# New durations in the planner of a fused linear-attention and two-MLP kernel

## The chip, the cores and the metric

The kernel runs on one core of a Trainium2 chip. Its time is the device time of one execution in microseconds (us). Before the change three runs took 1206.03, 1209.85 and 1210.98 us; the median is 1209.85 us. The profile is of one more execution, which took 1209.43 us.

## The reference

A recurrent attention over 4 x 8 heads, 768 steps, head size 40, feeds an MLP, and that feeds a second MLP. All is float32.

```python
for t in range(S):                      # state: B x H x D x D
    y[:, :, t] = einsum('bhd,bhde->bhe', r_t, state)
    Sa = einsum('bhde,bhe->bhd', state, a_t)
    state = state * w_t - outer(Sa, b_t) + outer(v_t, k_t)
x = y as 3072 tokens x 320
x = square(relu(x @ w_in))  @ w_out     # 320 -> 2048 -> 320
x = square(relu(x @ w_in2)) @ w_out2
```

## The kernel before

**The work.** The attention is computed in chunks of 32 steps. A slot n holds two such chunks (64 steps) of half of the batch; there are 24 slots. For each pair of slots the vector engine makes decay products with scans (`keys`, written into `w`, `sp`, `mm` or `kt`), multiplies them into `x` and `kb`, inverts small triangular matrices (`invert`: a block transpose into `p`, a first product from `lq` and `p`, fifteen steps on `mm`, a block transpose into `tt`), and transposes `kb` into `kt` (`values`). `chain` is the recurrence: for each of the two chunks of a slot TensorE runs small matmuls in the order `q,x` (result read out to `ss`), `ss,tt`, `q,lk`, `cs,q`, `r,ss`, each waiting for a copy or product of the one before on ScalarE or VectorE.

MLP 1 works on blocks of 256 tokens, one block for each pair of slots, 12 in all; MLP 2 has 12 blocks of the same size. A block has 16 steps. In MLP 1 a step is eight matmuls on `m_xh`, `m_xl` (in-step), a gate on ScalarE (relu, square, a rounding cast into `m_h`; the remainder `m_l` is made on VectorE or GpSimd), and eight matmuls on `m_h`, `m_l` (out-step). So each number is carried as two rounded parts. In MLP 2 the out-step has six matmuls of 320 columns. The weights come as raw 64-bit words and are decoded on the chip: `decode_w1` at the start, beside the first attention slots, and `decode_w2` after the last attention instruction, because the second weights lie where the attention's tiles lay. A decoded chunk takes two ScalarE multiplies and a rounding copy, three bit operations on VectorE, and two or three sums and products on VectorE or GpSimd.

**What sets the order.** All calls go through a recorder, `_Plan`. It keeps for each engine the time at which it would be free, by a table of costs, and gives the engine that is free first its ready task of the lowest priority number. Attention has the slot's number, the decode of the weights 2.7, gates -200, MLP matmuls 1000 and more: MLP matmuls fill the time in which no attention matmul is ready. The costs thus decide how many MLP matmuls stand between two attention groups in TensorE's queue, which the chip then runs strictly in that order. `cost` gives the time of a call on VectorE, ScalarE or GpSimd, `array` the cycles of a group of matmuls, `pe_time` turns these into time with a model of the clock, `taken` models the port that VectorE and GpSimd share. `either` records a call that two engines could do; `run` gives it to one of them by the same times. `plan.run("att")` plans until the last attention task; only then are the tasks of `decode_w2` and MLP 2 added.

Of the kernel before, what the change touches and what calls it, by code (L numbers as in the profile page):

```python
# [12 lines left out]
U32 = mybir.dt.uint32  # L13
# [59 lines left out]
class _Plan:  # L73
# [65 lines left out]
    def cost(self, eng, op, outs, ins):  # L139
        o = outs[0]  # L140
        n = 1
        for _, c in o.ap[1:]:
            n *= c
        if eng == "SP":
            return 690.0 if o.ap[0][1] in (32, 64) else 480.0
        psum = any(str(z.space).endswith("PSUM") for z in ins)
        if eng == "ACT":
            return (55 if psum else 93) + (90 if len(ins) > 1 else 0) + n / 1.2
        if eng == "POOL":
            return 149 + 2.1 * n if ins else 35 + 0.83 * n  # L150
        if op == "reciprocal":
            return 70 + n * 6.25
        if op == "tensor_reduce":
            n = 1
            for _, c in ins[0].ap[1:]:
                n *= c
        if op in ("tensor_copy", "tensor_scalar") and not psum:
            n /= 2
        return (64 + n) / 0.96

# [12 lines left out]
    def op(self, eng, name, fn, outs, ins, kw):  # L173
        cost = (2.0 if "is_transpose" in kw else 4.0) if eng.name == "PE" else self.cost(eng.name, name, outs, ins)
        rec = (eng.name, fn, cost, outs, ins, self.ports(eng.name, name, outs, ins))
        if self.open is not None:
            self.open.append(rec)
        else:
            self.add([rec])
# [12 lines left out]
    def add(self, ops, alts=None):  # L192
# [26 lines left out]
        if eng == "SP":  # L219
# [5 lines left out]
            nbytes *= max(1.0, 512 / run)  # L225
        k = self.array(ops) if eng == "PE" else None
        alts = alts or {eng: ([o[1] for o in ops], cost, max(o[5] for o in ops))}
        self.tasks.append((alts, self.prio, nbytes, self.tag, k))
        self.left[self.tag] = self.left.get(self.tag, 0) + 1
# [18 lines left out]
    def array(self, ops):  # L248

        cycles, columns, tiles, mode = 0, 0.0, [], None  # L250
        for _, _, passes, outs, ins, _ in ops:
            k, m = ins[0].ap[0][1], ins[0].ap[1][1]
            n = 1
            for _, c in outs[0].ap[1:]:
                n *= c
            r0, c0 = ins[0].offset // ins[0].ap[0][0], outs[0].offset // outs[0].ap[0][0]
            rows = 32 if k <= 32 else 64 if k <= 64 else 128
            cols = 32 if m <= 32 else 64 if m <= 64 else 128
            if rows == 128:
                r0 = 0  # L260
            mode = (rows, cols)
            if ins[0].dtype == F32R:
                cycles += max(n, 2 * m) + 6
                columns += n * m / 128
                tiles = []
                continue
            tile_ = (r0, c0)
            clash = [z for z in tiles if not (z[0] != r0 or z[1] != c0)] or (
                rows == 128 and any(z[1] == c0 for z in tiles)
            )  # L270
            if tiles and not clash:
                cycles += passes / 2 * m
                columns += passes * n * m / 128
                tiles.append(tile_)
            else:
                cycles += passes * max(n, m)
                columns += passes * n * m / 128
                tiles = [tile_]
        return mode, cycles, columns
# [29 lines left out]
    def taken(self, e, port, t, cost):  # L309

        if not port or e not in ("DVE", "POOL"):
            return t
        other = "POOL" if e == "DVE" else "DVE"
        until, what = self.held.get(other, (0.0, 0))
        if e == "DVE" and (port == 2 or what == 1) or e == "POOL" and (what == 2 or port == 1):
            t = max(t, until)
        self.held[e] = (t + cost, port)
        return t
# [963 lines left out]
```

## Time and profile before

| | |
|---|---|
| profiled execution | 1209.43 us |
| span of its instructions | 1207.6 us |
| TensorE busy | 1104.0 us (91%) |
| VectorE busy | 805.9 us (67%) |
| ScalarE busy | 747.5 us (62%) |
| GpSimd busy | 388.2 us (32%) |

In the table of stretches further down, the time from 0 to 140 us holds the start and the decode of the first weights, 140 to 716 us attention with MLP 1 in its gaps, 716 to 870 us the rest of MLP 1 beside the decode of the second weights, and the rest MLP 2 alone. A busy TensorE is not TensorE at its peak: matmuls overlap, and so the mean time of one is longer than the time between two.

### The profile page before, as it was taken

To read this page: it belongs to the slowest core of one execution; us is meant where nothing else is said; L and a number is where in the kernel's file an instruction comes from. 1 tells how busy PE (TensorE), PEld (TensorE's weight loads), DVE (VectorE), ACT (ScalarE), POOL (GpSimd) and SP (SyncE) were. 2 spreads that over 40 slices of the span, in tenths; PEclk is the share of its full clock that TensorE was granted. 3 is DMA by queue.
4 is the path that set the end of the run, shared out by engine and by line. 5 is a ranking of instruction groups with operands and counts; after the bars stand their busy time and mean duration, and the time that the engine had idled before them with its cause. 6 is when DMAs were issued, how large, how long until landed. Compare 5 with 4: busy or idle time off the path is not lost.

```text
span 1207.6 us, 43193 instructions
## 1 busy us (share of the span) xinstructions
PE 1104.0 (91%) x18096; PEld 1032.2 (85%) x18096; DVE 805.9 (67%) x1786; ACT 747.5 (62%) x2077; POOL 388.2 (32%) x443
## 2 busy tenths in 40 slices
PE   3888898998989998899899999999899999999996
PEld 2656787887878887798789899999899999999996
DVE  6887888789888978999798746666773232222221
ACT  4496554555565565556446468888666666666664
POOL 7544334223323332343224117776820000000000
PEclk9986789999998999999899999999899999999999
DMA  8555343155325515533451322332241010101000
GB/s 244 143 154 146 85 104 103 57 127 146 79 70 138 136 49 127 143 90 78 123 121 36 60 74 84 93 93 82 79 140 36 25 29 24 33 24 27 13 12 14
DMA packets 142239, 103.86 MB, mean 86 GB/s; under 512 B 98001, under 2 KB 110162, under 8 KB 142034
## 3 DMA queue, kind: packets, MB, share of 16 engines
q1 hardware_dynamic: 142034, 101.00, 31.5%
q8 instruction: 144, 2.36, 0.8%
q14 instruction: 61, 0.50, 0.1%
HBM read 82.88 MB, written 11.80 MB: 78 GB/s over the span
## 4 chain that ended last, share of the span: by engine, by line
PE 50%; DVE 7%; ACT 3%; issue 2%; DMA 1%; POOL 1%; SPq 1%; DVEq 0%; ACTq 0%; POOLq 0%
PE bank L69 50%; DVE mm L69 3%; DVE q L69 2%; ACT mm L69 1%; ACT q L69 1%; SPq L69 1%; DVE x L69 0%; DVE y L69 0%; DVE kt L69 0%; ACT m_h L69 0%; DMA v<-in_el_dram 0%; POOL kb L69 0%; DMA lk<-kt 0%; DVE p L69 0%; DMA mm<-in_win_dram 0%
## 5 line engine op out<-in xcount | busy, mean ns | idle before, releaser
L69 PE MATMUL bank<-m_xh,wi 128*128 128x256 f32 x1920 | 387.0, 286 | 9.7 <-ACT mm L69 5.4
L69 POOL TENSOR_TENSOR m_l<-mm,m_h 128x256 fp32r<-128x256 f32 x200 | 162.8, 816 | 546.3 <-ACT m_h L69 293.7
L69 PEld LDWEIGHTS bank<-m_xh,wi 128*128 128x128 f32 x1920 | 315.3, 193 | 13.2 <-ACT mm L69 6.0
L69 PE MATMUL bank<-m_xl,wi 128*128 128x256 f32 x1152 | 324.2, 285 | 1.8 <-POOL m_xl L69 1.8
L69 ACT ACTIVATE mm<-bank 128x256 f32<-128x256 f32 x384 | 146.2, 382 | 233.1 <-PE bank L69 214.3
L69 DVE TENSOR_TENSOR m_l<-mm,m_h 128x256 fp32r<-128x256 f32 x184 | 85.0, 462 | 217.6 <-ACT m_h L69 209.7
L69 PEld LDWEIGHTS bank<-m_xl,wi 128*128 128x128 f32 x1152 | 222.3, 193 | 2.3 <-POOL m_xl L69 2.3
L69 ACT ACTIVATE mm<-mm 128x256 f32<-128x256 f32 (+3 forms) x500 | 205.0, 423 | 30.6 <-POOL m_xl L69 14.8
L69 PE MATMUL bank<-m_h,wo 128*128 128x256 f32 x960 | 206.7, 297 | 0.1
L69 PE MATMUL bank<-wo,m_h 128*128 128x320 f32 x768 | 172.5, 311 | 1.7 <-ACT m_h L69 1.2
L69 PEld LDWEIGHTS bank<-m_h,wo 128*128 128x128 f32 x960 | 156.6, 192 | 10.0 <-issue 1.4
L69 PE MATMUL bank<-m_l,wo 128*128 128x256 f32 x576 | 156.6, 284 | 0.1
L69 ACT CAST m_h<-mm 128x256 fp32r<-128x256 f32 x359 | 145.1, 405 | 10.2 <-PE bank L69 1.9
L69 PEld LDWEIGHTS bank<-wo,m_h 128*128 128x128 f32 x768 | 125.7, 190 | 2.2 <-ACT m_h L69 1.4
L69 PE MATMUL bank<-wo,m_l 128*128 128x320 f32 x384 | 119.2, 310 | 1.0 <-POOL m_l L69 1.0
L69 DVE TENSOR_TENSOR mm<-mm 128x30 f32<-128x30 f32 (+9 forms) x317 | 106.0, 334 | 8.4 <-ACT wi L69 0.7
L69 PEld LDWEIGHTS bank<-m_l,wo 128*128 128x128 f32 x576 | 110.7, 192 | 0.5 <-POOL m_l L69 0.3
L69 DVE TENSOR_TENSOR q<-bank,cs 32x128 f32<-32x128 f32 (+1 forms) x240 | 87.7, 366 | 30.6 <-ACT q L69 22.2
L69 PE MATMUL bank<-q,lk 128*40 128x72 f32 x1536 | 63.7, 233 | 23.7 <-DVE q L69 10.6
L69 PEld LDWEIGHTS bank<-q,lk 128*40 128x40 f32 x1536 | 53.7, 120 | 31.7 <-ACT mm L69 9.9
L69 ACT COPY q<-bank 40x256 f32<-40x256 f32 (+1 forms) x168 | 54.6, 325 | 37.3 <-PE bank L69 33.6
L69 ACT ACTIVATE q<-bank 32x160 f32<-32x160 f32 x192 | 56.6, 295 | 27.3 <-PE bank L69 24.8
(135 smaller groups left out, 1633.1 us busy)
## 6 DMA issues: line engine op xcount, KB each, us to landing
kb<-in_el_dram SPq DMA_DIRECT2D x24, 512.0 KB
mm<-in_win_dram SPq DMA_DIRECT2D x30, 256.0 KB
a<-in_el_dram SPq DMA_DIRECT2D x24, 256.0 KB
v<-in_el_dram SPq DMA_DIRECT2D x24, 256.0 KB
r<-in_er_dram SPq DMA_DIRECT2D x24, 256.0 KB
lk<-kt SPq DMA_DIRECT2D x96, 64.0 KB
mm<-in_wr_dram SPq DMA_DIRECT2D x20, 260.0 KB
mm<-in_wout_dram SPq DMA_DIRECT2D x20, 256.0 KB
```

The lines of the kernel that those rows point to most:

```text
L69: self.plan.op(self, op, lambda: getattr(self.real, op)(*args, **kw), outs, ins, kw)
```

## The change

A few numbers of the planner change. No instruction is added or taken away; their order on all five engines changes, and which engine does what `either` leaves open.

```diff
-        if op in ("tensor_copy", "tensor_scalar") and not psum:
+        if op == "tensor_tensor_scan":
+            n *= 2.15
+        elif op == "transpose":
+            n = max(1.09 * n, 1.85 * min(n, 512))
+        elif o.dtype == U32:
+            n *= 1.2
+        elif op in ("tensor_copy", "tensor_scalar") and not psum:
             n /= 2
         return (64 + n) / 0.96
...
             if ins[0].dtype == F32R:
-                cycles += max(n, 2 * m) + 6
+                cycles += max(n, 2 * m) + 30
```

By these lines an MLP matmul of 256 columns is planned with 286 cycles instead of 262, a scan of 520 elements with 1231 ns instead of 608, the transpose of 512 elements with 1053 ns instead of 600, and a bit operation on 256 elements with 387 ns instead of 200 (one input) or 333 (two inputs).

Three places of the new order follow. The first is VectorE at the fifth of the twelve inversions, from the block transpose into `p` on. Before:

```order
L69 STREAM_TRANSPOSE p_115<-l_113 128x1024
L69 TENSOR_TENSOR q0_111<-bank0_67,cs_66 32x4x32 x3
L69 TENSOR_TENSOR y1_122<-bank2_69,w0_102 104x4x32
L69 TENSOR_TENSOR mm_81<-lq_114,p_115 128x16x32
L69 TENSOR_TENSOR q0_111<-bank0_67,w2_104 40x4x40
L69 TENSOR_TENSOR x1_106<-bank3_70,cs_66 32x512
```

Now:

```order
L69 STREAM_TRANSPOSE p_115<-l_113 128x1024
L69 TENSOR_TENSOR q0_111<-bank0_67,w2_104 40x4x40
L69 TENSOR_TENSOR q0_111<-bank1_68,w2_104 40x4x40
L69 TENSOR_TENSOR y0_121<-bank0_67,w2_104 104x4x32
L69 TENSOR_TENSOR q0_111<-bank1_68,w2_104 40x4x40
L69 TENSOR_TENSOR y1_122<-bank2_69,w0_102 104x4x32
```

The product from `lq` and `p` has left VectorE. The second place is GpSimd at the same inversion. Before:

```order
L69 TENSOR_TENSOR m_xl0_85<-mm_81,m_xh0_83 128x768
L69 TENSOR_TENSOR m_l0_90<-mm_81,m_h0_87 128x256
L69 TENSOR_TENSOR p_115<-p_115,mm_81 128x16x32
L69 TENSOR_TENSOR m_l1_91<-mm_81,m_h1_88 128x256
L69 TENSOR_TENSOR x2_107<-a_96,w2_104 64x512
```

Now:

```order
L69 TENSOR_TENSOR m_xl0_85<-mm_81,m_xh0_83 128x768
L69 TENSOR_TENSOR m_l1_91<-mm_81,m_h1_88 128x256
L69 TENSOR_TENSOR mm_81<-lq_114,p_115 128x16x32
L69 TENSOR_TENSOR p_115<-p_115,mm_81 128x16x32
L69 TENSOR_TENSOR m_l2_92<-mm_81,m_h2_89 128x256
```

The product stands here now, ahead of the sum into `p` that needs it. The third place is TensorE in the middle of attention, at the group of transposing matmuls `cs,q` of an odd slot (`q1`). Before:

```order
L69 MATMUL bank5_72<-m_xh1_84,wi1_125 128x256
L69 MATMUL bank5_72<-m_xh1_84,wi3_1_126 128x256
L69 MATMUL bank5_72<-m_xl1_86,wi3_1_126 128x256
L69 MATMUL bank2_69<-cs_66,q1_112 40x40 x16
L69 MATMUL bank1_68<-q0_111,lk0_108 40x72 x8
L69 MATMUL bank3_70<-sp_116,kb0_98 32x32 x32
```

Now:

```order
L69 MATMUL bank1_68<-q1_112,lk1_109 40x72 x8
L69 MATMUL bank0_67<-q0_111,lk0_108 40x72 x8
L69 MATMUL bank6_73<-m_h2_89,wo1_127 128x256 x2
L69 MATMUL bank6_73<-m_l2_92,wo1_127 128x256
L69 MATMUL bank2_69<-cs_66,q1_112 40x40 x16
L69 MATMUL bank1_68<-q0_111,lk0_108 40x72 x8
```

Between the second half of `q1,lk1` and `cs,q1` there were sixteen MLP matmuls, of which the last three are shown; now there are three and a small group of the other slot. Counted over the whole order, 2064 MLP matmuls stood ahead of the last attention matmul, and now 2168 do. By the attention group that they stand directly ahead of, `x,kb` has 519 instead of 434, `q,lk` 638 instead of 566, `ss,tt` 446 instead of 416, `cs,q` 245 instead of 323. Up to the last attention instruction VectorE has 1393 calls instead of 1400: three products into `kb` fewer, two into `x`, four from `lq`, one into `p`, one `m_xl`, and casts (three `m_h`, one `m_xh`, one `wo`), but one product into `sp` more, one `m_l`, and seven read-outs (two and four into `q`, one into `ss`). GpSimd has 285 instead of 268, among them seven `m_l` more.

## Rows read from the trace of the kernel before

**Rows 1.** Windows: busy us of each engine, PE clock, DMA, five stretches.

```profile
core 0: us, PE busy (x) PEld busy (x) DVE busy (x) ACT busy (x) POOL busy (x), PEclk, DMA share, GB/s
0.00:140.00 140.00, 97.21 (x1638) 75.90 (x1638) 113.66 (x284) 85.11 (x242) 73.33 (x82) 0.86 0.60 165
140.00:677.00 537.00, 490.62 (x11900) 446.43 (x11900) 464.24 (x1052) 302.87 (x874) 176.17 (x200) 0.95 0.39 99
716.00:870.00 154.00, 149.28 (x1219) 147.38 (x1220) 96.44 (x174) 125.74 (x359) 109.41 (x128) 0.98 0.31 91
870.00:1199.00 329.00, 328.48 (x2483) 328.08 (x2482) 107.93 (x214) 213.44 (x544) 25.66 (x29) 0.99 0.13 35
```

**Rows 2.** Chain that ended last, 480 to 600 us, share by line.

```profile
by line: PE bank L69 37.7%; DVE mm L69 12.5%; DVE q L69 10.0%; issue 9.0%; ACT q L69 4.7%; SPq L69 4.4%; DVE x L69 3.5%; DMA v<-in_el_dram 3.4%; ACT mm L69 2.1%; DVE p L69 2.0%; DVE kt L69 1.9%; DMA mm<-ys 1.9%; DVE y L69 1.7%; POOL p L69 1
```

**Rows 3.** The same chain after 670 us: start, us, what.

```profile
677.62 69.34 PE bank L69 x1121
748.21 83.12 PE bank L69 x707
...
854.61 1.00 DVE wi L69
855.62 2.69 DMA mm<-in_win_dram
...
868.71 329.78 PE bank L69 x2487
```

**Rows 4.** Groups on PE, 140 to 716 us: count, busy, mean ns, idle before.

```profile
L69 PE MATMUL bank<-q,lk 128*40 128x72 f32 x1408 | 58.3, 232 | 21.8 <-DVE q L69 8.7 <-ACT m_h L69 4.4 <-ACT mm L69 3.2
...
L69 PE MATMUL bank<-cs,q 40*40 40x40 f32 x1344 | 33.8, 204 | 1.8 <-DVE y L69 1.6
L69 PE MATMUL bank<-ss,tt 32*32 32x72 f32 x1408 | 32.0, 235 | 5.0 <-issue 1.5 <-DVE ss L69 1.1 <-ACT ss L69 0.9
```

**Rows 5.** Tile `lk` on PE: duration min/median/max, first and last start.

```profile
L69 PE MATMUL bank<-q,lk x1536: 223/226/342, 76.2 to 715.7; 128*40 128x72 f32 x192
```

**Rows 6.** Windows of 20 us in and after the rest of MLP 1.

```profile
780.00:800.00 20.00, 20.00 (x173) 20.00 (x173) 13.65 (x26) 15.75 (x45) 13.53 (x17) 1.00 0.27 77
...
860.00:880.00 20.00, 16.07 (x84) 14.92 (x85) 15.71 (x24) 13.13 (x36) 14.63 (x16) 0.74 0.39 108
```

**Rows 7.** Groups on VectorE, whole span, by shape.

```profile
L69 DVE TENSOR_TENSOR x<-a,w 64x512 f32<-64x512 f32 x17 | 24.0, 1413 | 0.6
...
L69 DVE TENSOR_TENSOR kb<-kb,mm 128x512 f32<-128x512 f32 x18 | 20.2, 1122 | 0.2
...
L69 DVE CAST m_h<-mm 128x256 fp32r<-128x256 f32 x25 | 7.3, 292 | 9.7 <-ACT mm L69 9.3 <-issue 0.2
```

**Rows 8.** Tile `lq` by engine: duration min/median/max.

```profile
L69 POOL TENSOR_TENSOR mm<-lq,p x6: 1046/1049/1052, 171.6 to 646.4; 128x512 f32<-128x512 f32 x6
L69 DVE TENSOR_TENSOR mm<-lq,p x4: 681/924/1248, 279.7 to 492.8; 128x512 f32<-128x512 f32 x4
```

**Rows 9.** Groups on GpSimd, whole span, by shape.

```profile
L69 POOL TENSOR_TENSOR m_l<-mm,m_h 128x256 fp32r<-128x256 f32 x200 | 162.8, 816 | 546.3 <-ACT m_h L69 293.7 <-DVE m_h L69 139.4 <-issue 64.2
L69 POOL TENSOR_TENSOR kb<-kb,mm 128x512 f32<-128x512 f32 x22 | 31.2, 1421 | 0.1
L69 POOL TENSOR_TENSOR x<-a,w 64x512 f32<-64x512 f32 x21 | 26.0, 1239 | 54.4 <-DVE w L69 32.5 <-PE bank L69 20.5 <-DMA a<-in_el_dram 1.2
```

**Rows 10.** Groups on ScalarE, 716 to 870 us, by shape.

```profile
L69 ACT ACTIVATE mm<-mm 128x256 f32<-128x256 f32 x86 | 35.1, 418 | 1.7 <-DMA mm<-in_win_dram 0.8
L69 ACT CAST m_h<-mm 128x256 fp32r<-128x256 f32 x76 | 30.5, 403 | 1.1 <-PE bank L69 0.2
L69 ACT ACTIVATE mm<-bank 128x256 f32<-128x256 f32 x77 | 29.1, 380 | 21.7 <-PE bank L69 17.5 <-POOL m_l L69 2.3 <-POOL dt L69 0.7
```

**Rows 11.** Timeline, 328.4 to 330.2 us: start, us, instruction.

```profile
328.61 1.16 DVE L69 STREAM_TRANSPOSE tt<-mm 128x512 f32<-128x512 f32 x1
...
329.81 0.28 PE L69 MATMUL bank<-m_xl,wi 128*128 128x256 f32 x1
...
330.02 0.39 PE L69 MATMUL bank<-ss,tt 32*32 32x72 f32 x12
```

**Rows 12.** Matmuls that split the first weights, whole span.

```profile
L69 PE MATMUL bank<-mm,cs 128*128 128x256 f32 x80 | 38.2, 570 | 1.1 <-DVE mm L69 1.1
```

## The prediction

> **What bounds the kernel now.** I read the stretches first, then the chain that ended last, then what TensorE waits for in attention. The stretches [rows 1] show two different kernels. From 870 us TensorE is busy 328.5 of 329 us at a granted clock of 0.99 (2.4 GHz all but throughout): MLP 2 alone, where the order has nothing to give. From 140 to 677 us no engine is full: TensorE 490.6 and VectorE 464.2 of 537 us, which leaves 46.4 us of TensorE idle. The chain says the same: between 480 and 600 us it lies on TensorE for 37.7% and on VectorE for 31.6% (12.5 + 10.0 + 3.5 + 2.0 + 1.9 + 1.7) [rows 2], the rest on ScalarE, DMA and issue. From 677.62 us on it is almost all TensorE [rows 3]; the last attention matmul starts at 715.7 us [rows 5].
>
> Then comes a hand-over. The decode of the second weights can only start there, and it has to be covered by what is left of MLP 1: 3072 - 2064 = 1008 matmuls. At 173 in 20 us [rows 6], 0.1156 us each, these are 116.5 us. They just fail to cover it: around 855 us the chain runs through the decode (a DMA of raw weights, sums on VectorE), and from 868.71 us TensorE runs to the end without a break [rows 3]. In the window 860 to 880 us TensorE is busy 16.07 of 20 us and its clock is 0.74, so part of it at 1.2 GHz [rows 6]. The end of the kernel is thus: end of attention, plus the decode (153 us, 715.7 to 868.7), plus 329.8 us of MLP 2, plus the tail.
>
> **The change part by part.**
>
> *More MLP matmuls in attention.* 104 more stand ahead of the last attention matmul: 104 x 0.1156 = 12.0 us of TensorE work that moves from behind 716 us to before it. If all of it found idle TensorE time, attention would end where it does; if none did, 12.0 us later. There is room: 46.4 us in all, and the largest single place is ahead of `q,lk`, where TensorE idles 21.8 us [rows 4] and where 72 of the new ones stand (638 against 566). But 30 more stand ahead of `ss,tt`, with only 5.0 us idle, and 85 ahead of `x,kb`; 78 fewer stand ahead of `cs,q`, with 1.8 us idle, where the group may now come early and wait. I take the chain's own share: added TensorE time lengthens attention by about 0.4 of it, +4.8 us (bounds 0 and 12.0).
>
> *Calls that leave VectorE in attention.* At the rows' means [rows 7, 8]: three products into `kb` at 1.12, two into `x` at 1.41, four from `lq` at 0.92 (the median) and three `m_h` casts at 0.29 us are 3.4 + 2.8 + 3.7 + 0.9 = 10.8 us. Against it stands one product into `sp` (as `x`, 1.4 us) and eight small calls; these I set off against the other casts and products that leave, each some 0.3 to 0.9 us, and lose 0.4 us more. Net 9.0 us off VectorE's 464. With VectorE's share of the chain, 0.3, this shortens attention by 2.7 us (bounds 0 and 9.0). GpSimd gets the products: 3 x 1.42 + 2 x 1.24 + 4 x 1.05 + 7 `m_l` x 0.82 = 16.7 us more [rows 8, 9] on an engine that is busy 176 of 537 us. I cost that at nothing; what hides it is GpSimd's idle time, and its price without that cover is a rival below. The read-outs that go from ScalarE to VectorE and the casts that come back leave ScalarE at 56% there: nothing.
>
> One page weighs against this part. The row from `lq` shows VectorE between 681 and 1248 ns for the same product, GpSimd always between 1046 and 1052 [rows 8]. The Trainium skill ("SBUF — State Buffer", section on practical consequences) says that a VectorE call with two inputs in SBUF and a GpSimd call that reads SBUF exclude each other for a whole instruction; by that rule the spread is VectorE waiting, the trace agrees, and each product on GpSimd can cost VectorE what it saved.
>
> *The end of attention.* Sum: +4.8 - 2.7 = +2.1 us; attention's last matmul at about 717.8 us (bounds: -9.0 and +12.0, so 706.7 to 727.7).
>
> *The hand-over.* MLP 1 has 904 matmuls left instead of 1008, 104.5 us. The decode then has less cover, and this would be worth 12.0 us of idle TensorE if the decode took its 153 us. But ScalarE does the decode and the gates of these same steps: 104 / 16 = 6.5 steps fewer in this stretch, each a relu at 0.380, a square at 0.418 and a cast at 0.403 us [rows 10], 1.20 us together. That is 7.8 us less on the engine that is busiest beside TensorE there (125.7 of 154 us; 17.5 us of its idle is waiting for TensorE's in-steps, and that too goes with the steps). I take the decode to be 7.8 us shorter. Bounds: 0, if the decode goes by its own chain through four buffers, and 12.0, if TensorE finds its weights as early as before relative to its need. VectorE and GpSimd have slack there (96 and 109 of 154 us). What is late next if the gates go is the DMA of raw weights, 2.69 us on the chain at 855 us [rows 3].
>
> *The start, the queues.* Up to 140 us attention's first groups stand ahead of up to ten matmuls that split the first weights (87 instead of 97 ahead of the fourth `q,x` group). By their row, 0.57 us each [rows 12], this is at most 5.7 us either way. VectorE is busy 113.7 of 140 us and DMA at 0.60 [rows 1], and neither gets less to do: I take 0 for it. SP's loads move with the tasks that they feed; in attention the chain has 3.4% on the load of `v` and 4.4% on SP's queue [rows 2], about 9 us in 120, and I take no change, with a few us either way inside the range.
>
> *Sum.* +2.1 - 7.8 = -5.7 us against the profiled execution's 1209.43 us (its span 1207.6 and 1.8 around it): 1203.7 us. The median of the runs is 0.4 us above that execution, so 1204 us.
>
> **The rivals.** *A, attention is bound by VectorE.* For it: every `ss,tt` wait is short, `q,lk` waits most for VectorE's `q` (8.7 us) [rows 4]. Then all 12.0 us go into idle time and the 9.0 us count in full: -9.0 - 7.8 = -16.8, 1193 us. Against it: TensorE's share of the chain is larger than VectorE's.
>
> *B, attention is bound by TensorE.* The 12.0 us count in full, VectorE's relief not at all: +12.0 - 7.8 = +4.2, 1214 us. For it: TensorE's 91% there, at a granted clock of 0.95.
>
> *C, the shared port.* The 16.7 us on GpSimd hold VectorE for as long: -9.0 + 16.7 = +7.7 us, of which 0.3 is +2.3; with +4.8 and -7.8 that is -0.7, 1209 us with the 0.4 to the median. Against it: GpSimd idles two thirds of attention, and a product ran at 681 ns on VectorE when it was alone. It is the mechanism of the page named above.
>
> *D, slower: TensorE comes late to the inverted matrix, and the decode keeps its length.* Once in each pair of inversions `ss,tt` of the even slot waits for the block transpose `tt`. At 328.61 + 1.16 = 329.77 us that ended, and TensorE came at 330.02 [rows 11]: matched within 0.3 us. At the five such places after 140 us there stand 32, 50, 56, 58 and 40 MLP matmuls directly ahead, now 58, 80, 48, 66 and 74: 90 more, 10.4 us, with no idle to take them. If `tt` is not later by as much, all of attention behind it is. With the decode at its 153 us that makes +10.4 us, 1220 us. It decides from the point where TensorE comes to these groups more than about 1 us after `tt`, and the decode is not shorter by the gates. Against it: fewer MLP matmuls elsewhere in the same period (`cs,q`) give part of it back.
>
> **How the numbers follow.** No difference is what lies within 0.5%, 1203.8 to 1215.9 us, about what a measurement of this kernel can tell. The forecast has 0.36: its own range is 1198 to 1209, from a decode shorter by 12.0 to one by 3, so 0.22 of it counts as faster and 0.14 as no difference. A has 0.20, faster. B has 0.13 (0.10 no difference, 0.03 slower, if the clock gives nothing back). C has 0.09, no difference. D has 0.22, slower. Faster 0.42, no difference 0.33, slower 0.25. The range goes from just below A's 1193 to just above D's 1220: 1192 to 1221 us.
>
> **What the profile would show.** The last `q,lk` at 716 to 720 us, with TensorE busier than 490.6 us per 537 before it; idle ahead of `q,lk` well under 21.8 us. Between that group and the last long run of TensorE about 145 us instead of 153. VectorE's busy time up to 677 us about 9 us lower, its `kb` and `lq` products not longer on average. The forecast is wrong if the last `q,lk` comes after 728 us, or if the distance from there to TensorE's last long run is still 153 us or more; the first speaks for B or D, the second for D alone. If the last `q,lk` comes before 710 us, A is right.

## The result, and the profile after

The changed kernel takes 1224.91 us (median of four runs, 1224.1 to 1227.64), the kernel before, run beside it, 1207.94 us: ratio 1.0144, 95% interval 1.011 to 1.0178. It is slower by 17 us; the forecast was 1204 us. The profiled execution after has a span of 1222.8 us, before 1207.6 us.

The first fence has stretches of the changed kernel, with the columns of [rows 1]; the first three answer to the same stretches there, the 20 us from 860 to the one in [rows 6].

```profile
140.00:677.00 537.00, 491.59 (x11682) 447.44 (x11682) 446.53 (x1019) 304.89 (x875) 186.78 (x213) 0.96 0.39 98
716.00:870.00 154.00, 148.30 (x1318) 144.17 (x1317) 90.87 (x165) 122.21 (x339) 100.17 (x117) 0.96 0.29 84
870.00:1199.00 329.00, 322.62 (x2406) 320.48 (x2407) 115.29 (x221) 211.09 (x541) 31.36 (x38) 0.98 0.14 38
840.00:860.00 20.00, 16.90 (x126) 16.58 (x125) 13.21 (x26) 16.03 (x46) 14.42 (x19) 0.97 0.31 91
860.00:880.00 20.00, 14.42 (x51) 12.18 (x52) 16.91 (x28) 12.08 (x33) 15.85 (x19) 0.50 0.38 105
880.00:900.00 20.00, 17.07 (x108) 15.63 (x107) 15.77 (x20) 9.49 (x25) 11.28 (x13) 0.85 0.54 160
838.00:900.00 62.00, 50.39 (x299) 46.38 (x298) 46.51 (x73) 39.57 (x107) 43.45 (x51) 0.78 0.41 120
```

And the last of these stretches in the kernel before:

```profile
838.00:900.00 62.00, 57.94 (x403) 56.53 (x402) 45.43 (x67) 43.69 (x118) 36.45 (x43) 0.92 0.40 119
```

Two things are to be seen. In attention (140 to 677 us) TensorE is as busy as before, 491.6 us, although VectorE lost 17.7 us (464.24 to 446.53) and GpSimd took 10.6. And between 838 and 900 us TensorE ran 299 matmuls instead of 403, at a mean granted clock of 0.78 instead of 0.92; from 860 to 880 us the clock is 0.50, so 1.2 GHz throughout, after 20 us in which TensorE was busy for 16.9.

The end of attention and the transposes `tt` of the inversions, by tile, in the changed kernel (duration, then first and last start) and, for `tt`, in the kernel before:

```profile
L69 PE MATMUL bank<-q,lk x1536: 222/226/341, 77.0 to 728.5; 128*40 128x72 f32 x192
L69 DVE STREAM_TRANSPOSE tt<-mm x10: 1045/1128/1159, 220.6 to 689.4; 128x512 f32<-128x512 f32 x10
```

```profile
L69 DVE STREAM_TRANSPOSE tt<-mm x10: 1003/1128/1161, 220.9 to 676.2; 128x512 f32<-128x512 f32 x10
```

The last `q,lk` starts at 728.5 us instead of 715.7 [rows 5]: 12.8 us later. The whole delay lies between the third and the twelfth `tt`, which are 468.8 us apart instead of 455.3. The groups of TensorE from 140 to 729 us (count, busy, mean ns, idle before) answer to [rows 4]:

```profile
L69 PE MATMUL bank<-q,lk 128*40 128x72 f32 x1408 | 55.9, 228 | 19.6 <-DVE q L69 10.0 <-ACT m_h L69 3.0 <-DVE y L69 2.9
...
L69 PE MATMUL bank<-cs,q 40*40 40x40 f32 x1344 | 34.7, 206 | 3.6 <-DVE y L69 3.1 <-issue 0.5
L69 PE MATMUL bank<-ss,tt 32*32 32x72 f32 x1408 | 31.4, 230 | 0.6 <-ACT ss L69 0.5
```

The idle time ahead of `q,lk`, where 72 more MLP matmuls stand, fell by 2.2 us only. Summed over TensorE's records from 140 us to the last `q,lk`, idle is 47.5 us, before 47.0: the added matmuls filled none of it.

The chain that ended last, of the changed kernel, answers to [rows 3]:

```profile
748.83 23.12 PE bank L69 x193
776.51 32.28 PE bank L69 x271
810.74 43.35 PE bank L69 x353
...
855.87 2.70 DMA mm<-in_win_dram
...
860.14 2.74 DMA mm<-in_win_dram
...
867.93 2.66 DMA mm<-in_win_dram
...
875.78 3.04 DMA dt<-in_wout_dram
...
882.86 5.06 DMA mm<-in_nat_dram
...
890.19 3.51 DMA mm<-in_nat_dram
...
896.87 315.16 PE bank L69 x2394
```

Where before one load of raw weights stood on it, there are four now, and behind them two loads of the input that the range check reads. The last run of TensorE without a break begins at 896.87 us instead of 868.71.

### The profile page after: what moved, and what is told of

Same layout as the page of the kernel before. It is cut to its first block, busy times and chain, and to the rows that moved or that the text cites. A ratio compares the mean times of both kernels' runs of the same rounds, so it can differ in the third digit from the quotient of the medians.

```text
span 1222.8 us, 43187 instructions
## 1 busy us (share of the span) xinstructions
PE 1105.0 (90%) x18096; PEld 1029.7 (84%) x18096; DVE 801.0 (66%) x1773; ACT 752.0 (61%) x2078; POOL 400.5 (33%) x455
## 4 chain that ended last, share of the span: by engine, by line
PE 43%; DVE 5%; DMA 2%; ACT 2%; issue 1%; POOL 1%; SPq 0%; DVEq 0%; ACTq 0%; POOLq 0%
PE bank L69 43%; DVE mm L69 2%; DVE q L69 1%; ACT mm L69 1%; DMA mm<-in_nat_dram 1%; DMA mm<-in_win_dram 1%; DMA w<-in_wl_dram 0%; SPq L69 0%; DVE y L69 0%; DMA lk<-kt 0%; DMA dt<-in_wout_dram 0%; POOL dt L69 0%; DVE sp L69 0%; ACT q L69 0%; DVE cs L69 0%
## 5 line engine op out<-in xcount | busy, mean ns | idle before, releaser
L69 POOL TENSOR_TENSOR m_l<-mm,m_h 128x256 fp32r<-128x256 f32 x197 | 156.5, 796 | 539.1 <-ACT m_h L69 404.5
L69 ACT ACTIVATE mm<-mm 128x256 f32<-128x256 f32 (+2 forms) x500 | 206.7, 424 | 42.5 <-DMA mm<-in_win_dram 10.5
L69 ACT CAST m_h<-mm 128x256 fp32r<-128x256 f32 x371 | 150.3, 406 | 9.8 <-PE bank L69 0.5
L69 DVE TENSOR_TENSOR mm<-mm 128x30 f32<-128x30 f32 (+8 forms) x316 | 100.4, 318 | 8.5 <-ACT wi L69 0.8
L69 PEld LDWEIGHTS bank<-wo,m_l 128*128 128x128 f32 x384 | 73.1, 190 | 4.6 <-POOL m_l L69 2.6
L69 ACT COPY q<-bank 40x160 f32<-40x160 f32 (+1 forms) x162 | 52.6, 325 | 38.7 <-PE bank L69 36.5
```

What stands on the lines that cost most here:

```text
L69: self.plan.op(self, op, lambda: getattr(self.real, op)(*args, **kw), outs, ins, kw)
```

## The experiments

All edits are to the planner's numbers unless it is said otherwise. A flag `new` switches a cost at the line `plan.run("att")`, so that the order up to attention's last task ("early") and the order behind it ("late") change apart. One table has the milestones of the profiles: the start of the last `q,lk`, the start of the last `m_h,wo` matmul (the end of MLP 1) and the end of the last write into `wi` (the last of the second weights' `wo` follows 2 to 8 us behind). "Lag" is the last `wi` write less MLP 1's end. "Rest" is the time from MLP 1's end to the end of TensorE's last `wo,m_h` matmul: MLP 2, always the same instructions. Each line is of a single execution, which can lie some us from the median of its kernel's runs (late_new's is 6 us above).

| kernel | last q,lk | MLP 1 ends | last wi | lag | rest | ratio (95%) |
|---|---|---|---|---|---|---|
| before | 715.7 | 838.4 | 868.7 | 30.3 | 359.9 | 1 |
| after | 728.5 | 839.0 | 882.8 | 43.8 | 375.5 | 1.0144 (1.011 to 1.0178) |
| early_new | 732.5 | 844.9 | 876.6 | 31.7 | 361.9 | 1.0112 (1.0075 to 1.0149) |
| late_new | 715.9 | 837.0 | 881.5 | 44.5 | 376.5 | 1.0095 (1.0066 to 1.0125) |
| pe30 | 714.2 | 866.7 | 860.6 | -6.1 | 351.5 | 1.0143 (1.0072 to 1.0214) |
| dve | 738.2 | 849.8 | 899.3 | 49.5 | 378.9 | 1.0255 (1.0184 to 1.0325) |
| late_u32 | 712.8 | 833.9 | 879.2 | 45.3 | 375.5 | 1.0096 (1.0068 to 1.0123) |
| late_pe | 712.8 | 836.0 | 866.2 | 30.2 | 360.6 | 1.0016 (0.9981 to 1.0052) |
| scan | 747.6 | 845.0 | 891.1 | 46.1 | 375.2 | 1.0201 (1.0115 to 1.0287) |
| tp | 720.1 | 836.7 | 869.0 | 32.3 | 362.7 | 1.0014 (0.9974 to 1.0055) |
| dfirst | 714.7 | 863.8 | 842.3 | -21.5 | 351.7 | 1.0177 (1.0123 to 1.0231) |
| late_cheap | 708.1 | 831.7 | 848.5 | 16.8 | 350.7 | 0.9894 (0.9859 to 0.9928) |
| early_cheap | 736.3 | 852.7 | 867.1 | 14.4 | 351.7 | 1.0103 (1.002 to 1.0186) |

Lag and rest go together in every line. With a lag up to 16.8 us the rest takes 351 us (350.7 to 351.7); at 30 to 32 us it takes 360 to 363, at 44 to 46 us 375 to 377, at 49.5 us 379. So the kernel's end is MLP 1's end, plus 351 us, plus what the lag costs. By this the changed kernel lost 0.6 us at MLP 1's end and 15.6 us in the rest, of the 16.2 us by which TensorE ends later.

### Which half of the order costs: early_new, late_new

```diff
 # early_new: new = True at first; late_new: new = False at first
-        if op in ("tensor_copy", "tensor_scalar") and not psum:
+        if self.new and op == "tensor_tensor_scan":
...
     plan.run("att")
+    plan.new = False   # late_new: True
```

> The new costs hold for everything recorded up to the last attention task (attention, decode of the first weights, MLP 1) and the old ones for what is recorded behind it (decode of the second weights, MLP 2). 2168 MLP matmuls stand ahead of the last attention matmul, as in the changed kernel. Theory T (lost cover: the attention goes at TensorE's pace, 104 more MLP matmuls ahead of its end put that end 12 to 13 us later, MLP 1 ends when it did, and the decode of the second weights then leaves TensorE without work for as much longer): last q,lk at about 728 us, time 1221 to 1227 us. Rival R (the new order of decode and gates behind attention, and the range check's reads, are what costs): last q,lk at 728 us too, but time 1208 to 1213 us.

> The other way round: old costs up to the last attention task, new ones behind it. 2064 MLP matmuls ahead of the last attention matmul, as before. Theory T: last q,lk at 716 us, time 1205 to 1212 us, as before. Rival R: 1219 to 1227 us.

Each half alone costs about 1%: 1218.49 and 1217.56 against 1205.59 us. No range of either theory holds the measured times: early_new lies between T's and R's, late_new just under R's. The idea that attention's end carries the loss alone fell with late_new, whose attention ends as before (715.9 us). In early_new attention ends 16.8 us later, and the decode behind it takes 144.1 us (732.5 to 876.6) instead of 153.0: the relief that the prediction counted is there, 8.9 us against its 7.8; 70 gates fall into it instead of 76. In late_new the decode takes 165.6 us, 12.6 us more, with attention and the number of matmuls left as before. Together, in the changed kernel, it takes 154.3 us: one cancels the other. The two losses do not seem to add up, 1.1 and 0.95% against 1.4%, but this is hardly clear of the intervals.

### Which of the late costs: late_u32, late_pe

```diff
 # late_u32: new = True from plan.run("att") on (no scan or transpose is left there);
 # MLP matmuls stay at + 6
+        elif self.new and o.dtype == U32:
+            n *= 1.2
 # late_pe: that branch off, and + 30 for MLP matmuls from there on
```

> Old costs, but the new cost of bit operations (387 instead of 200 or 333 ns) for what is recorded behind attention: the decode of the second weights. Theory U (planned longer, the bit operations move back in VectorE's queue behind calls that wait for ScalarE; a buffer of raw weights is then held 19.0 us instead of 17.7, eight times over, and the decode ends 10 to 13 us later): reuse of a buffer 18.5 to 19.5 us, chunks begun by 838 us 24 or fewer, time 1215 to 1222 us. Rival M (the 30 cycles of MLP 2's matmuls move the gates): 1204 to 1210 us, reuse 17.7 us.

> Old costs, but 30 cycles for the matmuls recorded behind attention (MLP 2). Theory U: as before, 1204 to 1210 us, reuse of a buffer 17.5 to 18 us. Rival M: 1215 to 1222 us.

The planned time of the three bit operations is enough for all of the late loss; 30 cycles for the matmuls, behind attention, change nothing that can be measured. What VectorE waited for between 716 and 870 us (us in total, times, longest), kernel before and late_u32:

```profile
DVE m_l L69 <- ACT m_h L69: 12.3, 9, 4.0
DVE mm L69 <- ACT mm L69: 7.2, 8, 2.3
```

```profile
DVE m_l L69 <- ACT m_h L69: 17.4, 11, 3.4
DVE mm L69 <- ACT mm L69: 14.8, 10, 2.8
DVE dt L69 <- ACT wi L69: 6.0, 3, 3.6
```

Planned as longer, a bit operation is put later in VectorE's queue, behind calls that wait for ScalarE. From the start of the second ScalarE multiply of a chunk to the start of the bit operation that needs it pass 4.11 us on average over the 36 chunks, before 2.71. The four raw-weight buffers are held that much longer: from one load into a buffer to the next pass 19.05 us instead of 17.7, and the loads run behind. The issues of loads on SP from `in_wout`, kernel before and late_u32:

```profile
L69 SPq DMA_DIRECT2D dt<-in_wout_dram x8: 327/328/424, 719.2 to 863.8; - x8
```

```profile
L69 SPq DMA_DIRECT2D dt<-in_wout_dram x8: 327/328/423, 716.3 to 871.6; - x8
```

The first of them is 2.9 us earlier than before and the last 7.8 us later.

### The other direction: late_cheap

```diff
 # new = True from plan.run("att") on
+        elif self.new and o.dtype == U32:
+            n *= 0.125
```

> Old costs up to the end of attention; behind it the bit operations are planned with 100 ns, shorter than the 200 or 333 of before. Theory U (the shorter they are planned, the earlier they stand in VectorE's queue and the shorter a buffer of raw weights is held): reuse of a buffer under 17.5 us, second multiply to bit operation under 2.7 us, time 1199 to 1205 us. Rival N (no such relation, 200 ns happened to give a good order): 1206 to 1216 us.

If the planned time acts as a place in the queue, a time that is far too short must help. It does: 1192.0 against 1205.79 us, ratio 0.9894 (0.9859 to 0.9928). This is the fastest version, ahead of both kernels, and below the range that theory U gave. The same views as above, and the window from 838 us:

```profile
DVE m_l L69 <- ACT m_h L69: 5.8, 10, 1.1
DVE mm L69 <- ACT mm L69: 3.4, 3, 2.0
```

```profile
L69 SPq DMA_DIRECT2D dt<-in_wout_dram x8: 328/328/424, 711.5 to 841.4; - x8
```

```profile
838.00:900.00 62.00, 62.00 (x474) 62.00 (x473) 38.51 (x59) 42.13 (x111) 25.54 (x31) 1.00 0.35 98
```

With the bit operation planned at 100, 200 (333 with two inputs) and 387 ns the time from the multiply's start to its own is 2.10, 2.71 and 4.11 us, a buffer goes round in 15.4, 17.7 and 19.05 us, and the rest takes 350.7, 359.9 and 375.5 us. TensorE is full and at 2.4 GHz through the hand-over. The rest is 9.2 us shorter; another 6.7 us in this profile lie ahead of MLP 1's end, where attention's order is that of before: I take this for the spread of single executions, which is not shown (in six other profiles with that order of attention the last `q,lk` lies between 712.8 and 715.9 us).

### The decode ahead of everything: dfirst

```diff
-        plan.prio = P_D
+        plan.prio = -300.0
```

> The kernel before, with the decode of the second weights put ahead of the gates in priority. Theory H (what is lost between 838 and 870 us before, 4 us idle and 10 us at half the clock, is waiting for the second weights): a buffer is reused after under 16 us, the loss goes, time 1198 to 1204 us. Rival G (the gates of MLP 1 come late instead and TensorE idles between 716 and 838 us): 1208 to 1220 us.

The loads go as fast as in late_cheap, and the decode ends early, at 842.3 us. But the time is 1225.69 us, above both ranges, by the mechanism of rival G: MLP 1 ends 25.5 us later, since its gates now wait behind the decode. TensorE is busy 85.5 of the 100 us from 740 us on (before 99.3), and 9.3 us of its idle time there end with a `m_l` of GpSimd. The loss at the hand-over is gone, and a larger one stands in its place.

### Which of the early costs: pe30, dve, scan, tp

```diff
 # pe30: this line alone
-                cycles += max(n, 2 * m) + 6
+                cycles += max(n, 2 * m) + 30
 # dve: the three branches on scans, transposes and U32 alone
 # scan: n *= 2.15 alone; tp: the transpose branch alone
```

> Only the 30 cycles for an MLP matmul, the VectorE costs as before. 1822 MLP matmuls stand ahead of the last attention matmul, 242 fewer than before. Theory T: at 0.1156 us each the attention ends up to 28 us earlier, last q,lk at 688 to 700 us; the decode of the second weights is covered, TensorE idles under 2 us between 800 and 900 us and stays at 2.4 GHz there; the time is that of before less its 9 us of hand-over loss plus what TensorE idles more in attention: 1198 to 1206 us. Rival V (the attention goes at VectorE's pace): last q,lk at 712 to 718 us, the 28 us of matmuls become idle time, time 1215 to 1230 us.

> Only the new VectorE costs (scans, transposes, bit operations), MLP matmuls as before with 6 cycles. 2152 MLP matmuls ahead of the last attention matmul, 88 more than before. Theory T: last q,lk about 10 us later, 724 to 728 us, time 1217 to 1223 us. Rival V: last q,lk at 712 to 718 us, time 1205 to 1211 us.

> The kernel before with the new cost of scans alone (1231 instead of 608 ns). 2288 MLP matmuls ahead of the last attention matmul, 224 more than before. Theory T with a knee at about 2064 (every matmul beyond it lengthens attention by its own 0.1156 us): from the third to the twelfth inversion 470 to 482 us instead of 455, last q,lk 732 to 742 us. Rival P (the place counts, not the number): 455 to 465 us.

> The kernel before with the new cost of block transposes alone (1053 instead of 600 ns for 512 elements). 2112 MLP matmuls, 48 more. Theory T with a knee: 458 to 463 us between the third and the twelfth inversion, last q,lk 718 to 722 us. Rival P: 465 us or more, since it is the transpose that TensorE's ss,tt waits for that is planned longer.

The new costs pull both ways: longer matmuls make the planner put 242 fewer MLP matmuls ahead of attention's end (1822 instead of 2064), longer scans 224 more (2288), transposes 48 more (2112); all together it is the 104 of the change. In pe30 attention ends only 1.5 us earlier, as rival V had it, and the 242 matmuls come behind it: MLP 1 ends 28.3 us later, though the hand-over costs nothing. More than 2064 matmuls lengthen attention. The transposes `tt` in scan, third to twelfth (its time is the median of two runs, 1229.01 us):

```profile
L69 DVE STREAM_TRANSPOSE tt<-mm x10: 1027/1137/1169, 228.5 to 709.7; 128x512 f32<-128x512 f32 x10
```

They are 481.2 us apart, 25.9 more than before; 224 x 0.1156 is 25.9. That the two agree to a tenth is luck: 214 of the 224 stand between these transposes, and a lower clock and less idle time there change the sum as well. In tp they are 4.7 us further apart, where 48 x 0.1156 is 5.5; that is inside the spread of before's order (454.8 to 461.2 us over eight profiles) and shows nothing by itself. The last `q,lk` of scan (747.6 us) and both marks of dve lie beyond every range that was expected.

The number of matmuls is not all that differs. From 140 to 677 us, in pe30, dve and scan, with the columns of [rows 1]:

```profile
140.00:677.00 537.00, 476.36 (x11689) 429.31 (x11691) 465.01 (x1060) 287.56 (x831) 175.05 (x191) 0.93 0.40 99
140.00:677.00 537.00, 490.87 (x11649) 447.31 (x11649) 430.64 (x990) 302.12 (x871) 203.92 (x223) 0.93 0.40 99
140.00:677.00 537.00, 492.06 (x11479) 450.43 (x11480) 428.92 (x978) 298.41 (x852) 184.97 (x210) 0.93 0.39 97
```

The granted clock is 0.93 in all three, against 0.95 before and 0.96 in the changed kernel. So TensorE's time from 140 us to the last `q,lk` is best split into idle time, busy time at 1.2 GHz, and the rest. In the kernel before, an in-step matmul begins 117 ns behind the one ahead of it at 2.4 GHz and 213 ns at 1.2 GHz (medians of 881 and 41 pairs). By this about 0.45 of the busy time at 1.2 GHz is what the lower level costs; that is an estimate, as it takes the other matmuls to scale alike. Differences to the kernel before, in us:

| kernel | MLP matmuls (x 0.1156) | last q,lk | idle | busy at 1.2 GHz (x 0.45) | rest of the busy time |
|---|---|---|---|---|---|
| pe30 | -242 (-28.0) | -1.5 | +14.7 | +20.5 (+9.2) | -25.4 |
| tp | +48 (+5.5) | +4.4 | +1.3 | -9.0 (-4.1) | +7.2 |
| after | +104 (+12.0) | +12.8 | +0.5 | -9.2 (-4.1) | +16.4 |
| early_new | +104 (+12.0) | +16.8 | +2.3 | -2.5 (-1.1) | +15.6 |
| dve | +88 (+10.2) | +22.5 | +1.8 | +17.9 (+8.1) | +12.6 |
| scan | +224 (+25.9) | +31.8 | +0.7 | +14.7 (+6.6) | +24.5 |

Added matmuls find no idle time in any of these orders, and they cost about their own time. In pe30 fewer matmuls left TensorE idle and at a lower clock instead. So the order before stood at a corner: its 47 us of idle time in attention are not to be had by more MLP matmuls. On top of that the clock takes up to 8 us or gives up to 4 back: in dve it is most of what 88 matmuls do not account for. What made the clock differ was not tested.

### Is it the number of columns: before_thin, after_thin

```diff
-                T.matmul(h, z, x, start=(i == 0), stop=(i == 7))
+                thin = w is w1 and i in (1, 4, 7)
+                T.matmul(h, z, x, start=(i == 0), stop=(i == 7), thin=thin)
```

`thin` halves the columns that the matmul moves on the chip, while the planner still counts all. It saves less than was expected. From 742 to 830 us, where MLP 1 runs alone on TensorE, a step of eight takes 868 instead of 933 ns (medians of 18 steps), so 65 ns less and not three times 58: the matmul behind a thin one begins 60 ns after it instead of 117, but the next one 172 ns later instead of 117. The 130 and 136 steps ahead of attention's end thus save about 9 us, not 23.

> The same thinning of MLP 1's in-steps in the kernel before, in its own order. Theory T with a knee (the kernel before stands where TensorE and VectorE just balance, as fewer MLP matmuls did not end attention earlier): last q,lk at 708 to 716 us, with the saved time as idle TensorE time. Theory T without a knee: 692 to 700 us.

> The changed kernel in its own order on every engine, but three of the eight in-step matmuls of MLP 1 (those on the second part of the input) move 128 instead of 256 columns: half of that term is left out. About 400 of them stand before the end of attention, at most 0.058 us less each, 23 us less TensorE work there. Theory T (attention goes at TensorE's pace in the changed kernel): last q,lk at 728 less 10 to 20, 708 to 718 us. Rival V (it goes at VectorE's pace): 725 to 729 us.

In before's order idle time of TensorE grew from 47.0 to 52.7 us, the last `q,lk` is at 712.9 us, and one run took 1207.68 us. This fits the flat side of the corner, but 9 us are near the spread of this order (708.1 to 715.9 us), so the sign is weak. In the changed order attention should have come back and did not: `q,lk` at 740.1 us, beyond both ranges, and 1234.63 us. The window says why the run can't decide it:

```profile
140.00:677.00 537.00, 489.63 (x11500) 449.95 (x11501) 442.16 (x993) 298.72 (x853) 187.01 (x213) 0.93 0.39 98
```

With less to do TensorE is as busy as in the changed kernel, because its granted clock is 0.93 instead of 0.96. Up to the last `q,lk` it was busy for 72.6 us at 1.2 GHz instead of 42.1; at 0.45 that is 13.7 us, and idle time grew by 4.6 us. The rest of its busy time did shrink, by 6.7 us. One execution each, inconclusive for the changed order.

### Is it the reload of x: before_noys, after_noys

In attention of the changed kernel ScalarE waits 16.1 us for the reload of attention's output, before 5.4 us. The edit reads MLP 1's blocks from an input array instead, and so leaves out the hand-over of attention's result.

```diff
-        load_x(ys[at, 0:256]..., ys[at, 256:320])
+        load_x(ys[at, 0:256]..., ys[at, 256:320], at if isinstance(at, int) else None)   # real source: el
```

> The same replacement in the kernel before. Theory Y: at most the 5.4 us that ScalarE waits there, last q,lk 711 to 716 us, time 1202 to 1208 us. Rival O: 714 to 717 us, time 1206 to 1210 us.

> The changed kernel in its own order, but MLP 1 reads its input blocks from an input array of the same shape that is there from the start, instead of attention's stored output; the hand-over of attention's result to MLP 1 is left out. ScalarE waits for these loads 16.1 us in attention in the changed kernel, 5.4 us before. Theory Y (these waits stand in ScalarE's queue ahead of attention's read-outs and are the 12.8 us): last q,lk at 714 to 721 us instead of 728, time 1214 to 1220 us. Rival O (the places of the MLP matmuls and of VectorE's scans in the new order): last q,lk 726 to 730 us, time 1222 to 1227 us.

Before's order does not care (1.0018, 0.9996 to 1.0041). The changed order became slower still, 1237.86 against 1205.79 us (1.0262, 1.0211 to 1.0314), with ScalarE's wait at 12.1 us and `q,lk` at 751.2 us, beyond the ranges of both theories. Most of what came on top goes with a lower clock again:

```profile
140.00:677.00 537.00, 487.80 (x11348) 444.73 (x11348) 427.65 (x967) 291.75 (x832) 181.19 (x206) 0.92 0.40 98
```

Up to the last `q,lk` TensorE was busy for 86.3 us at 1.2 GHz, in the changed kernel for 42.1. At 0.45 that is 19.9 of the 22.7 us by which this attention ends later than the changed kernel's. That the reload is the cause is not supported; as the wait hardly went away, it is not refuted either.

### Both halves put together: early_cheap

```diff
+        elif o.dtype == U32:
+            n *= 1.2 if self.new else 0.125     # new until plan.run("att")
```

> The changed kernel's costs up to the end of attention (2168 MLP matmuls ahead of it), and behind it old costs with the bit operations at 100 ns. Theory: attention stays long (last q,lk 726 to 734 us), the decode of the second weights takes 125 to 140 us from there instead of 154, TensorE loses nothing at the hand-over, time 1196 to 1205 us: the two parts of the change are separate. Rival: a later start of the decode with less cover brings the loss back, 1208 to 1216 us.

The decode takes 130.8 us and the hand-over costs nothing (rest 351.7 us), as expected. The time, 1215.32 us, is not: attention ends 20.6 us later, 8 us more than in the changed kernel with the same order, and MLP 1 ends 14.4 us later. The time falls into the rival's range, but not by the loss that the rival named. Without the hand-over's loss a longer attention is seen at the end.

## Why the prediction was wrong

**The end of attention (step: +4.8 - 2.7 = +2.1 us).** Failed. I took the chain's share of TensorE, 0.4, as the part of the added work that counts. None of it found idle time: +12.8 us measured against 12.0 for 104 matmuls, just beyond the bound that I had set, and +16.8 and +20.6 us in two more profiles of the same order of attention (early_new, early_cheap). That 12.8 lies so near to 12.0 is in part luck: the clock gave about 4.1 us back in this execution, and the rest of the busy time grew by 16.4 us, 4.4 more than the matmuls account for. The share of a chain in one stretch is no price for work that is added to a queue that runs strictly in order. VectorE's relief was twice what I counted (17.7 us against 9.0) and attention ended later all the same, so rival A is out.

**GpSimd's work (step: at nothing).** Held. It took 10.6 us more in attention, not 16.7, and rival C does not show: the products that the prediction priced did not become longer where they stayed on VectorE. Changed kernel, whole span, against [rows 7]:

```profile
L69 DVE TENSOR_TENSOR x<-a,w 64x512 f32<-64x512 f32 x15 | 20.5, 1363 | 1.9 <-DMA a<-in_el_dram 1.5
...
L69 DVE TENSOR_TENSOR kb<-kb,mm 128x512 f32<-128x512 f32 x15 | 16.4, 1095 | 0.2
```

The mean is 1363 instead of 1413 ns and 1095 instead of 1122. (The remainder `m_xl` became longer, 1005 ns over 11 calls instead of 958 over 13.) The Trainium skill ("SBUF — State Buffer", section "Who interferes with whom") says that a VectorE call with two inputs in SBUF contends with a GpSimd call that reads SBUF. The trace of the kernel before agrees: of two `kb` products that overlap one is longer, 673 ns on VectorE beside 1744 on GpSimd or 1694 beside 1192, where the shortest are 672 and 1178. But more work on GpSimd did not make it bite harder.

**The hand-over (step: -7.8 us).** Failed, and by about as much as the first step: from the last `q,lk` to the last `wi` write pass 154.3 us where I had counted on 145. The relief is real (8.9 us in early_new). What the sum left out is that the same change gives the decode itself a new order, and late_u32 shows that the bit operations' planned time alone costs more than the relief (its decode takes 166.4 us, before 153.0). I had bounded the step by 0 and 12.0, with no loss in it, though a changed order can lengthen a decode as well as shorten it.

**What a late decode costs.** The sum had 1 us for each us. The runs give 0 up to a lag of 16.8 us, about 9 us at 30 and about 25 us at 44. Between 838 and 900 us idle grew from 4.1 to 11.6 us, 7.5 of the 15.6 us. Another part is the clock: its mean fell from 0.92 to 0.78, by the records from 10.2 to 27.3 us at 1.2 GHz. TensorE was busy in 8.9 and 18.9 us of these; at 0.45 the 10.0 more are 4.5 us. Some 3.6 us are left open. The range check adds to the idle time; VectorE from 887.9 us in the changed kernel:

```profile
887.95 2.21 DVE L69 TENSOR_REDUCE cs<-mm 128x1 f32<-128x960 f32 x2 [2.31 <-DMA mm<-in_nat_dram]
890.08 0.28 DVE L69 CAST m_h<-mm 128x256 fp32r<-128x256 f32 x1
...
893.72 1.15 DVE L69 TENSOR_REDUCE cs<-mm 128x1 f32<-128x960 f32 x1 [1.24 <-DMA mm<-in_nat_dram]
...
896.25 0.57 DVE L69 CAST m_h<-mm 128x256 fp32r<-128x256 f32 x1
```

Casts that MLP 2 needs stand behind reductions that wait for their load. Moving the check alone was not tried.

**The rivals.** The two marks that the prediction set for being wrong both came: the last `q,lk` after 728 us, and 153 us or more from there (154.3 to the last `wi` write, 168.4 to the last long run of TensorE). D came closest, 1220 us for a late attention and a decode that keeps its length. But its mechanism is not what is seen. TensorE comes to `ss,tt` 0.1 to 0.8 us after the five transposes that it named, as before (0.1 to 0.9): `tt` itself came later by as much. What is right in it is the place: from the third transpose on, the four stretches that end in one of these are 21.2 us longer, the five others together 7.8 us shorter. And the decode kept its length for a reason that D did not have, two effects that cancel. B's price for attention (12.0) came nearest, with the luck told above; its relief at the hand-over did not come.

**The size.** TensorE's 12.0 us that moved into attention were not lost: MLP 1 ends 0.6 us later, as fewer matmuls are left (6.5 us later in early_new, whose attention took 4.0 us more). Nearly all of the loss, 15.6 of 16.2 us, lies where the decode, which cannot start before attention ends, no longer lies under MLP 1.

**Open.** Single executions of one order of attention differ by up to 7.8 us: the last `q,lk` at 728.5, 732.5 and 736.3 us in three profiles of the changed order (after, early_new, early_cheap), and from 708.1 to 715.9 us in those of before. In the three it is idle time (47.5, 49.3 and 52.0 us) and busy time at 1.2 GHz (42.1, 48.8 and 50.6 us); what is left of the busy time is the same within 1 us. What sets the idle time and the clock was not found, nor what the 4 us are by which the changed order keeps TensorE busy beyond its 104 matmuls.

## What to carry to other kernels

A cost in a greedy planner is a place in a queue, not only a duration: durations nearer to the trace's (the transpose planned with 1053 ns, measured with 1128 in the median) made this kernel 1.4% slower, and 100 ns instead of the 200 or 333 of before for the calls that free a scarce buffer made it 1.1% faster. Filler that is moved ahead of a hand-over lengthens a full queue by its own time; that time is saved behind the hand-over, but it is gone as cover for what starts there. Switch such a change on and off at the hand-over, and read the two halves apart: their sum hides that one of them pays for the other. And before a longer stretch is put down to added work, split TensorE's time into idle, busy at either clock level, and the rest.

## What the runs showed of the hardware

Fewer columns did not make a row of matmuls faster in proportion. With the second, fifth and eighth of eight in-step matmuls at 128 instead of 256 columns, the times from one start to the next at 2.4 GHz were 118, 60, 172, 118, 59, 172, 116 and 58 ns, before about 117 each (before_thin, 742 to 830 us): what came early behind a thin matmul was lost again one matmul later, except at the end.

The granted clock can undo what an edit saves. In the changed order the same edit had a mean granted clock of 0.93 instead of 0.96 from 140 to 677 us, by two levels 75 instead of 43 us at 1.2 GHz, and attention ended 11.6 us later (one execution each). In before's order it left the clock at 0.96, before 0.95, and attention's end 2.8 us earlier. In dve the whole-execution clock was low in all four runs, 0.928 to 0.938, where 19 runs of the kernel before beside it had 0.951 to 0.966.
